# Sigmoid attention and token/channel mixer on one core: accumulating the first batch's token sums in PSUM, laying x back by DMA, permuting on GpSimd, and PSUM banks kept in two-bank tiles

## Chip, cores and metric

One core of one Trainium2 chip. The metric is the device time of one execution in microseconds. With one core, a run over 1.5% above the fastest of the same kernel counts as slow. The span of a profile is about 2 us shorter than the time of that run (398.9 for one of 400.8 before).

Engine names: PE is the TensorE matmul, PEld its weight load, DVE VectorE, ACT ScalarE, POOL GpSimd, SPq the queue of SyncE that issues the plain and the transposing DMAs. POOL issues the loads that cast from float32 to float16.

## The reference, cut to what matters

```python
# q, k, v: (8 batches, 12 heads, 448 tokens, 64); float32
scores = matmul(q, k.T) / 8 - log(448)
attn   = 1 / (1 + exp(-scores))
x      = heads side by side of matmul(attn, v)         # (8, 448, 768)
h      = relu(x.T @ w_tok1) @ w_tok2                   # along tokens, 448 -> 256 -> 448
u      = x + h.T
out    = u + relu(u @ w_ch1) @ w_ch2                   # along channels, 768 -> 1536 -> 768
```

Attention of a later batch and the mixer of an earlier one run side by side, so that PE, which has most of the work, always has some.

## The kernel before: the parts that matter here

A planner in the kernel simulates all engines, picks an order, and then emits the instructions in that order, which gives a list for each engine. A buffer is a `Buf`; it has a few slots, and each slot gets one tile:

```python
    def ap(self):
        if self.tile is None:
            pool = self.plan.pools[self.space]
            self.tile = pool.tile(
                self.shape, self.dtype, tag=f"{self.tag}{self.slot}", bufs=1, name=self.name
            )
        return self.tile
    ...
    def bank(name, shape, dtype=FP32):                       # four single PSUM banks, tag "m"
        return plan.buf("m", 4, shape, dtype, "psum", name)
    ...
    # scores: two slots of two banks
    ps = plan.buf("qk", 2, [128, 2, 512], FP32, "psum", ...)
```

A load brings four heads as rows of 448 elements, heads `2h+s` on partition half `s`:

```python
    nc.gpsimd.dma_start(
        out=t.ap().rearrange("r h j e -> r h (j e)"),
        in_=src[b, 4 * m : 4 * m + 4].rearrange("(h s) (p j) e -> (s p) h (j e)", s=2, j=J),
    )
```

The attention output comes out transposed. PE lays it back, eight 128x128 transposes for each group of four heads ("B"), and DVE copies the result to x. For batch 0, the token mixer (`K1`, relu, `K2`), the add to x, and a PE transpose ("U") lead to `uT`, the input of the first channel matmul ("C1"):

```python
    def back(pb=pb, xt=xt):
        for s in range(2):
            for jj in range(4):
                ...
                nc.tensor.transpose(out=pb[:, jj, :, s, :], in_=xt[:, s, c : c + 128], identity=ident[:, :])
    ...
    # C1: six matmuls of 448 columns into one bank, then a relu by DVE that empties the bank
    nc.tensor.matmul(out=ps[:, :], lhsT=w_ch1[...], rhs=uT[b][:, db, :], start=(db == 0), stop=(db == NDB - 1))
    nc.vector.tensor_scalar(out=h2aT[b][:, cb, :], in0=ps[:, :], scalar1=0.0, scalar2=None, op0=MAX)
```

## Time and profile before

| | before |
|---|---|
| time, median of the runs beside the changed kernel | 402.95 us (401.63 to 406.11) |
| span of the profile | 398.9 us |
| PE busy | 371.8 us, 93% |
| first score matmul | 9.6 us |
| first channel matmul (C1) | 42.8 us |
| PE waits for DVE, summed over the table of waits | 0.9 us |

From the page of the kernel before. Part 1 gives busy time and share of the span; part 2 cuts the span into 40 slices, where a digit is the busy share in tenths:

```profile
PE 371.8 (93%) x3368; PEld 197.1 (49%) x3368; DVE 181.1 (45%) x416; ACT 213.6 (54%) x271; POOL 63.4 (16%) x95
...
PE   2898999199799999999999999999999999999995
...
DMA  7969999978934598548845798638321252031143
```

The dip of PE in slice 8 is the one long stop after the start. The table of PE's waits names it, in the first line here (us in total, times, longest). Slice 11, at seven tenths, holds a shorter stop of 1.9 us, for the tail cast (ACT's float16 copy of `u_tail`, the last 64 tokens of u).

```profile
PE qk L416 <- DMA qT<-qp: 8.6, 1, 8.6
PE tk L371 <- DMA k<-in_k_dram: 7.1, 3, 5.1
```

The DMA queues (packets, MB, share of 16 engines' span), and one line of the windows (us, then busy time of PE, PEld, DVE, ACT and POOL with instruction counts, granted clock, DMA share, GB/s):

```profile
q0 software_dynamic: 24112, 21.93, 35.9%
q1 hardware_dynamic: 54784, 23.41, 30.0%
```

```profile
200.00:250.00 50.00, 50.00 (x443) 26.42 (x442) 21.53 (x53) 29.24 (x38) 6.42 (x9) 1.00 0.75 136
```

PE is busy for 50 of 50 us there, at a DMA share of 0.75. A share of 1 is not the most that this count can reach: from 70 to 80 us it was 1.28.

### The profile page before, as it was taken

Reading aid. Unit: us, or ns where it says so; the run is one execution under the profiler, and the core shown is the slowest. Engines: PE = TensorE matmul, PEld = TensorE weight load, DVE = VectorE, ACT = ScalarE, POOL = GpSimd, SP = SyncE. Lnnn points to the kernel's source line nnn. Section 1 sums busy time; section 2 is a strip of 40 time slices with the busy share of each in tenths; the row PEclk is TensorE's granted clock in tenths of the full one; section 3 lists DMA queues with packets and bytes.
Section 4 is the critical chain, followed back from the end, with each engine's and each line's share of the span. In section 5 each row is a group of like instructions: output and inputs, shape, how many; then the busy total and the mean of one; then the engine's idle time right before and its main releaser. Section 6 shows DMA issues by size and latency. Waiting matters only on the chain.

```text
span 398.9 us, 8001 instructions
## 1 busy us (share of the span) xinstructions
PE 371.8 (93%) x3368; PEld 197.1 (49%) x3368; DVE 181.1 (45%) x416; ACT 213.6 (54%) x271; POOL 63.4 (16%) x95
## 2 busy tenths in 40 slices
PE   2898999199799999999999999999999999999995
PEld 1555454055445554455455554545454554555553
DVE  3377545146544434464442544463342432755321
ACT  1996774167655756586634758476646764220000
POOL 8393325002202022202220012200000000000000
PEclk9999999799999999999999999999999999999999
DMA  7969999978934598548845798638321252031143
GB/s 106 204 102 205 208 208 200 194 112 124 165 63 76 111 197 152 89 88 155 128 73 124 121 187 167 103 67 129 70 48 39 62 114 58 19 63 29 39 109 90
DMA packets 78931, 45.83 MB, mean 115 GB/s; under 512 B 52528, under 2 KB 75248, under 8 KB 78896
## 3 DMA queue, kind: packets, MB, share of 16 engines
q0 software_dynamic: 24112, 21.93, 35.9%
q1 hardware_dynamic: 54784, 23.41, 30.0%
q8 instruction: 26, 0.43, 0.4%
q14 instruction: 9, 0.07, 0.1%
HBM read 43.84 MB, written 11.01 MB: 138 GB/s over the span
## 4 chain that ended last, share of the span: by engine, by line
PE 84%; DMA 10%; POOL 3%; issue 1%; ACT 1%; DVE 0%; POOLq 0%; ACTq 0%
PE c L710 28%; PE c L742 24%; PE qk L416 9%; PE xa L447 7%; PE yn L647 5%; PE k L549 5%; PE c L751 4%; DMA qT<-qp 4%; DMA k<-in_k_dram 3%; PE xb L485 2%; DMA w_tok_s<-in_moe_w_tok_dram 2%; DMA v<-in_v_dram 2%; POOL k L265 1%; POOL w_tok L301 1%; POOL q L265 1%
## 5 line engine op out<-in xcount | busy, mean ns | idle before, releaser
L431 ACT ACTIVATE attn<-qk,att_bias 128x896 f16<-128x896 f32 x168 | 161.5, 1007 | 94.4 <-PE qk L416 94.3
L710 PE MATMUL c<-uT,w_ch 128*128 128x448 f16 x576 | 118.8, 353 | 0.0
L742 PE MATMUL c<-w_ch,h2aT 128*128 128x384 f16 x576 | 100.7, 329 | 0.0
L722 DVE TENSOR_SCALAR h2aT<-c 128x448 f16<-128x448 f32 x96 | 59.9, 624 | 79.8 <-PE c L710 79.6
L710 PEld LDWEIGHTS <-w_ch 128*128 128x128 f16 x576 | 53.0, 98 | 55.5 <-issue 11.9
L742 PEld LDWEIGHTS <-h2aT 128*128 128x128 f16 x576 | 55.8, 99 | 40.9 <-issue 5.6
L416 PE MATMUL qk<-qT,kT 64*64 64x448 f16 x672 | 51.9, 370 | 10.9 <-DMA qT<-qp 8.6
L766 DVE TENSOR_TENSOR u<-u,c 128x384 f32<-128x384 f32 x48 | 26.6, 554 | 65.6 <-PE c L742 65.4
L265 POOL DMA_DIRECT2D v<-in_v_dram x24 | 17.2, 719 | 179.0 <-PE xa L447 164.7
L447 PE MATMUL xa<-attn,v 64*64 64x448 f16 x672 | 36.3, 350 | 0.0
L474 ACT ACTIVATE xT<-xa 128x448 f16<-128x448 f32 x43 | 21.1, 545 | 23.4 <-PE xa L447 23.4
L416 PEld LDWEIGHTS <-kT 64*64 64x64 f16 x672 | 14.4, 105 | 37.6 <-issue 35.4
L447 PEld LDWEIGHTS <-v 64*64 64x64 f16 x672 | 19.4, 107 | 12.9 <-issue 2.6
L659 DVE TENSOR_TENSOR u<-x,yn 128x384 f32<-128x384 f16 x42 | 21.5, 550 | 5.6 <-PE yn L647 5.6
L647 PE MATMUL yn<-h,w_tok 128*128 128x384 f16 x112 | 23.5, 328 | 0.0
L549 PE MATMUL k<-x,w_tok 128*128 128x384 f16 (+1 forms) x102 | 21.2, 318 | 0.0
L669 ACT ACTIVATE u<-u 128x768 f16<-128x768 f32 x21 | 17.6, 845 | 5.5 <-DVE u L659 5.5
L566 ACT ACTIVATE h<-k 128x384 f16<-128x384 f32 (+1 forms) x30 | 14.4, 484 | 9.8 <-PE k L549 9.8
L265 POOL DMA_DIRECT2D q<-in_q_dram x24 | 17.3, 719 | 9.6 <-PE xa L447 3.3
L265 POOL DMA_DIRECT2D k<-in_k_dram x24 | 17.3, 721 | 8.6 <-DMA w_ch<-in_moe_w_ch_dram 6.9
L394 DVE COPY qp<-q 128x384 f16<-128x384 f16 (+1 forms) x54 | 10.9, 266 | 14.4 <-DMA qT<-qp 9.5
L549 PEld LDWEIGHTS <-w_tok 128*128 128x128 f16 x136 | 12.2, 98 | 10.8 <-issue 4.5
(58 smaller groups left out, 192.2 us busy)
## 6 DMA issues: line engine op xcount, KB each, us to landing
out_dram<-u SPq DMA_DIRECT2D x48, 192.0 KB, 2.9
k<-in_k_dram POOLq DMA_DIRECT2D x24, 224.0 KB, 6.0
q<-in_q_dram POOLq DMA_DIRECT2D x24, 224.0 KB, 7.0
v<-in_v_dram POOLq DMA_DIRECT2D x24, 224.0 KB, 4.7
w_ch<-in_moe_w_ch_dram POOLq DMA_DIRECT2D x6, 768.0 KB, 16.4
out_dram<-ut SPq DMA_DIRECT2D x8, 192.0 KB, 2.9
uT<-u SPq DMA_TRANSPOSE x24, 2.8
kT<-kp SPq DMA_TRANSPOSE x18, 3.1
```

The source lines that it names most:

```text
L265: nc.gpsimd.dma_start(out=t.ap().rearrange("r h j e -> r h (j e)"), in_=src[b, 4 * m : 4 * m + 4].rearrange("(h s) (p j) e -> (s p) h (j e ...
L416: nc.tensor.matmul(out=ps[64 * s : 64 * s + 64, h, 0:S], lhsT=kT[64 * h : 64 * h + 64, i, s, :], rhs=qT[64 * h : 64 * h + 64, :, s, :], st ...
L431: nc.scalar.activation(out=at[:, :, :], in_=ps[:, :, 0:S], func=SIGMOID, bias=bias_t[:, :], scale=att_scale,)
L447: nc.tensor.matmul(out=ps[s][64 * h : 64 * h + 64, :], lhsT=vf[64 * s : 64 * s + 64, h, order[i], :], rhs=attn[i][64 * s : 64 * s + 64, h, :],
L474: nc.scalar.activation(out=xt[:, s, :], in_=ps[s][:, :], func=COPYF)
L549: nc.tensor.matmul(out=ps[:, :], lhsT=w_tok1[:, slot, 128 * t : 128 * t + 128], rhs=XT[b][:, c] if jj == 3 else X[b][:, jj, c], start=(jj ...
L647: nc.tensor.matmul(out=ps[:, :], lhsT=w_tok2[:, t, s0 : s0 + 2, :], rhs=h1[:, t, c], start=(t == 0), stop=(t == 1),)
L659: nc.vector.tensor_tensor(out=utile[rows, c] if blk == 3 else u[b][:, blk, c], in0=XT[b][rows, c] if blk == 3 else X[b][:, blk, c], in1=ps ...
L710: nc.tensor.matmul(out=ps[:, :], lhsT=w_ch1[cb // 4][:, db, 128 * (cb % 4) : 128 * (cb % 4) + 128], rhs=uT[b][:, db, :], start=(db == 0), ...
L722: nc.vector.tensor_scalar(out=h2aT[b][:, cb, :], in0=ps[:, :], scalar1=0.0, scalar2=None, op0=MAX)
L742: nc.tensor.matmul(out=ps[:, :], lhsT=h2aT[b][:, cb, 128 * blk : 128 * blk + 128], rhs=w, start=(cb == 0), stop=(cb == NCB - 1),)
L766: nc.vector.tensor_tensor(out=t, in0=t, in1=ps[:, :], op=ADD)
```

## The change

It is meant to shorten the start and to take work from PE and DVE:

- Batch 0: the token sums are matmuls that go on accumulating on the attention output in PSUM (`start=False`), so that one copy gives `uT`. The plain `u` of batch 0 is made later.
- Batches 2 to 7: x is laid back by two transposing DMAs per four heads, issued from SP.
- The permutes of q and k (copies that reorder token groups, before a DMA transposes them) move from DVE to GpSimd, the spreading of `w_tok2` (copies into the layout that K2 reads) from GpSimd to DVE, the token relus from ACT to DVE.
- Batch 0 is loaded in pieces, by head of a pair; turns (the PE transposes of q and k) and scores of the very first heads are cut by head too.
- The planner gets a model of how late DMAs are, and one store of eight PSUM banks that serves pairs ("wide") and single banks.

```diff
+    def banks(self, pool, kept):
+        pair = self.slot // 2
+        if pair not in kept:
+            kept[pair] = pool.tile([128, 2, 512], FP32, tag=f"banks_{pair}", bufs=1, name=f"banks_{pair}")
+        if self.tag == "wide":
+            self.tile = kept[pair]
+            return self.tile
+        t = kept[pair][:, self.slot % 2, :]
+        ...
+            first, n = (6, 7, 5, 4) if self.spare or self.wide == 2 else (6, 7), 1
+        ...
+                b.slot = min(got, key=lambda x: (max(x[0], t), x[1]))[2]
@@ load_qkv, batch 0
+            view = heads.rearrange("(s h) (p j) e -> h s p (j e)", s=2, j=J)
+            for h in range(2):
+                    nc.gpsimd.dma_start(out=t[:, h, :, :].rearrange("r j e -> r (j e)"), in_=view[h])
@@ turned / attention
-                            nc.vector.tensor_copy(out=pm[:, to, :, :], in_=src[:, fr, :, :])
+                    nc.gpsimd.tensor_copy(out=pm[:, to, :, :], in_=src[:, fr, :, :])
+            if b >= 2:
+                for s in range(2):
+                        nc.sync.dma_start_transpose(out=X[b][:, :, cols[s]], in_=xt[:, s, :])
+                continue
@@ batch 0
+                        nc.tensor.matmul(out=ps[s](every), lhsT=h1[0][:, t, ...], rhs=w_tok2[:, t, 0:J, :],
+                            start=False, stop=(t == 1), skip_group_check=True)
... (most of the diff is cut)
```

## The prediction

> **What bounds it now.** The page's engine totals and slices show TensorE (PE) at 93% busy, ACT 54%, DVE 45%, POOL 16%, and the chain of waits is 84% PE work. From 104 to 394 us PE never stops (windows: 80.0 of 80 us, 100.0 of 100 us), so there only removed PE work counts. Time is lost in three places:
> - 0 to 43 us. First score matmul at 9.6 us, first channel matmul at 42.8 us. At warm rates from the chain (8 scores 0.50 us, 28 value matmuls 1.32, 8 transposes 0.45) its PE work is about 27 us, so 16 us are waits. ACT sets the pace to 31 us (21 sigmoids of 1.0 us); then PE waits for k loads until 32.4 and 40.7.
> - 64 to 78 us: PE waits 8.6 us for the transposed q of batch 2 (the table of waits), late because loads saturate the DMA (share 1.2 from 30 to 80 us). The DMA was idle at 20 to 30 us (0.67): POOL waited 4.4 us for w_tok2 and spread it for 3.7 us before issuing more loads.
> - 100 to 104 us: about 2 us for the tail cast of batch 1.
>
> **What the change does.**
> 1. Batches 2 to 7 no longer lay x back with PE: 18 groups of 8 transposes at 0.45 us = -8.1 us, nearly all on the critical path. DVE loses 18 x (0.55 + 0.28) = 15 us, off path. Instead 36 SP transposes of 128x512 run; scaled from the present 128x896 ones (SP issue 1.3 us, landing 3 us): about 0.8 us issue, 2 to 4 us landing. Mean DMA share rises from 0.65 to about 0.72 in the middle: affordable.
> 2. Batch 0: K2, add, PE transpose, copy become 12 matmuls of 448 columns accumulating on the attention output, then one copy. PE: -24 at about 0.11 us, -24 transposes (1.35 us), +12 x 0.19, +16 x 0.16 later (the plain sums, filled in behind): about +1 us. Latency from last sigmoid to first channel matmul falls by 2 to 3 us. [...]
> 3. Start: half loads put the first score near 7.5 us (-2). Spread moves to DVE, so POOL keeps issuing; loads of weights and batch 2 land about 5 us earlier, and the new model of DMA lateness places batch 2's scores later. I expect first channel matmul near 36 us, startup waits -5 us, and the 8.6 us wait nearly gone (-7.5).
> 4. Permutes: 25 us leave DVE (off path); on POOL, by its present copies (784 ns at 128x384, 381 ns at 128x128), 1.95 us each, 70 us over 36: POOL to 30 to 35%. Off path.
> 5. Token relus ACT to DVE: may ease the 2 us at 100 us (-1).
>
> **Sum.** -8.1 - 7.5 - 5 - 1 + 1 = about -20.5; give back 1 for late x transposes: 398.9 to about 379.5 us span, time 382 us (time exceeds span by 2.9 now).
>
> Range 375 to 392. Faster by over 2%: 0.94; within: 0.05; slower: 0.01.
>
> **Right or wrong.** Right if PE busy falls to about 360 us; first score 7 to 8 us; first channel matmul 34 to 38; no wait over 3 us for qT; no K1 wait on x transposes; POOL near 130 us busy. Wrong if bursts of loads and X transposes queue on SP so that K1 or scores wait, or if POOL permutes delay later load issues.

## More of the kernel before

The timeline at the first channel matmuls (start, duration, engine, what; in brackets the idle time of that engine before it, and what ended it):

```profile
42.77 2.44 PE L710 MATMUL c<-uT,w_ch 128*128 128x448 f16 x12
...
44.12 0.62 DVE L722 TENSOR_SCALAR h2aT<-c 128x448 f16<-128x448 f32 x1 [0.57 <-PE c L710]
...
45.15 0.57 PE L416 MATMUL qk<-qT,kT 64*64 64x448 f16 x8
...
45.26 0.62 DVE L722 TENSOR_SCALAR h2aT<-c 128x448 f16<-128x448 f32 x1 [0.51 <-PE c L710]
...
45.55 1.49 PE L447 MATMUL xa<-attn,v 64*64 64x448 f16 x28
```

Two chains of six matmuls fill two banks. The first relu starts at 44.12 us, as soon as the first chain is done and while the second still runs. PE goes on without a bracket: it waits for nothing.

## The result

| | before | after |
|---|---|---|
| time, median | 402.95 us | 507.58 us (505.76 to 510.10) |
| ratio, fast runs | | 1.2587, 95% interval 1.2489 to 1.2684 |
| span | 398.9 us | 505.8 us |
| PE busy | 371.8 us, 93% | 393.2 us, 78% |
| first score, first channel matmul | 9.6, 42.8 us | 13.2, 57.0 us |
| PE waits for DVE | 0.9 us in 2 waits | 77.8 us in 122 waits |

A ratio is the mean time of one kernel's fast runs over that of the other's of the same rounds, so not quite the ratio of the medians that are quoted. The changed kernel was slower by a quarter where a gain of 5% had been forecast.

The lines of the page of the changed kernel that answer to those above:

```profile
PE 393.2 (78%) x3204; PEld 203.2 (40%) x3204; DVE 157.0 (31%) x294; ACT 209.1 (41%) x253; POOL 109.9 (22%) x206
...
PE   1888888887877967797779976987788986966774
...
DMA  7999999948884995689534995262213431210123
```

After the start, where the first turn comes at 9.0 us, no stop is longer than 4.4 us. PE is at seven or eight tenths in nearly every slice: the loss is spread evenly, so it comes from something that happens all the time. The waits of PE say what:

```profile
PE banks L839 <- DVE h2aT L864: 30.9, 44, 0.9
PE banks L481 <- DMA k<-in_k_dram: 9.7, 2, 9.0
PE banks L884 <- DVE u L908: 8.8, 14, 0.7
PE banks L560 <- DVE h2aT L864: 7.2, 10, 0.7
PE banks L839 <- DMA uT<-u: 7.1, 3, 4.4
```

Matmuls of every kind wait some 0.7 us for a DVE operation that empties a bank. L839 is C1, L884 the second channel matmul, L560 the value matmul; a value matmul has no data from `h2aT`, so that wait can only be for room. The timeline at the first channel matmuls:

```profile
59.60 2.43 PE L839 MATMUL banks<-uT,w_ch 128*128 128x448 f16 x12 [0.74 <-DVE h2aT L864]
61.96 0.57 PE L524 MATMUL banks<-qT,kT 64*64 64x448 f16 x8
62.07 1.16 DVE L864 TENSOR_SCALAR h2aT<-banks 128x448 f16<-128x448 f32 x2 [2.52 <-PE banks L839]
...
63.28 2.43 PE L839 MATMUL banks<-uT,w_ch 128*128 128x448 f16 x12 [0.74 <-DVE h2aT L864]
```

Compare with the same place before. The relu of the first chain does not start when that chain is done (about 60.8 us, half of the 2.43 us), but when both are, at 62.07, after 2.52 us of idleness; and the next pair of chains waits until both relus are done. DVE is no slower (622 ns a relu, 624 before) and much idler. Two banks work in lockstep that have nothing to do with each other.

PE's busy time also rose, by 21.4 us with 164 fewer matmuls. Two runs below account for parts of it: with own tiles it is 13.2 us less (e1: 380.0 us), and without the cut by head 7.6 us less again (e13: 373.9 us, e10: 381.5 us).

The DMA queues, and the first loads (out<-in, KB each, median us from issue to landing):

```profile
q0 software_dynamic: 40384, 21.99, 33.7%
q1 hardware_dynamic: 74368, 28.13, 29.6%
...
k<-in_k_dram POOLq DMA_DIRECT2D x6, 112.0 KB, 8.5
```

The same bytes of loads take 16,272 packets more, and the halves of batch 0, at 112 KB, take longer than the 224 KB loads before (median 6.0 us for k).

### The profile page after: what moved, and what is told of

It is laid out like the page before. It is cut to its first block, busy times and chain, and to the rows that moved or that the text cites. A ratio compares the mean times of both kernels' runs of the same rounds, so it can differ in the third digit from the quotient of the medians.

```text
span 505.8 us, 7716 instructions
## 1 busy us (share of the span) xinstructions
PE 393.2 (78%) x3204; PEld 203.2 (40%) x3204; DVE 157.0 (31%) x294; ACT 209.1 (41%) x253; POOL 109.9 (22%) x206
## 4 chain that ended last, share of the span: by engine, by line
PE 61%; DVE 20%; DMA 11%; ACT 3%; issue 3%; POOL 1%; DVEq 0%; POOLq 0%
PE banks L839 24%; PE banks L884 18%; DVE h2aT L864 10%; PE banks L560 6%; PE banks L762 4%; DVE u L908 4%; DMA uT<-u 4%; PE banks L732 3%; DVE u L783 3%; PE banks L893 2%; DMA w_tok<-in_moe_w_tok_dram 2%; DMA k<-in_k_dram 2%; DMA v<-in_v_dram 2%; PE banks L524 2%; DMA x<-xT 2%
## 5 line engine op out<-in xcount | busy, mean ns | idle before, releaser
L539 ACT ACTIVATE attn<-banks,att_bias 128x896 f16<-128x896 f32 (+1 forms) x172 | 161.7, 987 | 128.9 <-PE banks L524 128.5
L839 PE MATMUL banks<-uT,w_ch 128*128 128x448 f16 x576 | 124.6, 359 | 44.4 <-DVE h2aT L864 30.9
L884 PE MATMUL banks<-w_ch,h2aT 128*128 128x384 f16 x576 | 100.7, 326 | 15.2 <-DVE u L908 8.8
L864 DVE TENSOR_SCALAR h2aT<-banks 128x448 f16<-128x448 f32 x96 | 58.4, 622 | 140.8 <-PE banks L839 108.8
L839 PEld LDWEIGHTS <-w_ch 128*128 128x128 f16 x576 | 56.1, 99 | 107.6 <-issue 65.8
L884 PEld LDWEIGHTS <-h2aT 128*128 128x128 f16 x576 | 55.9, 97 | 57.6 <-issue 22.5
L524 PE MATMUL banks<-qT,kT 64*64 64x448 f16 x672 | 55.0, 375 | 1.9 <-ACT attn L539 1.8
L908 DVE TENSOR_TENSOR u<-u,banks 128x384 f32<-128x384 f32 x48 | 26.1, 551 | 87.5 <-PE banks L884 45.0
L560 PE MATMUL banks<-attn,v 64*64 64x448 f16 x672 | 39.4, 361 | 12.9 <-DVE h2aT L864 7.2
L593 ACT ACTIVATE xT<-banks 128x448 f16<-128x448 f32 x43 | 21.6, 543 | 60.9 <-PE banks L839 32.8
L560 PEld LDWEIGHTS <-v 64*64 64x64 f16 x672 | 23.2, 109 | 27.0 <-issue 19.0
L762 PE MATMUL banks<-h,w_tok 128*128 128x384 f16 x128 | 27.6, 326 | 7.7 <-DVE u L783 5.2
L783 DVE TENSOR_TENSOR u<-x,banks 128x384 f32<-128x384 f16 x48 | 24.8, 550 | 25.9 <-PE banks L762 15.2
L732 PE MATMUL banks<-x,w_tok 128*128 128x384 f16 x112 | 20.5, 326 | 6.3 <-DVE h L744 2.5
```

The source lines that it names most:

```text
L524: nc.tensor.matmul(out=ps[64 * s : 64 * s + 64, h, 0:S], lhsT=kT[64 * h : 64 * h + 64, i, s, :], rhs=qT[64 * h : 64 * h + 64, :, s, :], st ...
L539: nc.scalar.activation(out=at[:, hs, :], in_=ps[:, hs, 0:S], func=SIGMOID, bias=bias_t[:, :], scale=att_scale,)
L560: nc.tensor.matmul(out=ps[s](slice(64 * h, 64 * h + 64)), lhsT=vf[64 * s : 64 * s + 64, h, order[i], :], rhs=attn[i][64 * s : 64 * s + 64, ...
L732: nc.tensor.matmul(out=ps[:, :], lhsT=w_tok1[:, w1_slot(side, blk), 128 * t : 128 * t + 128], rhs=X[b][:, x_block(side, blk), c], start=(b ...
L762: nc.tensor.matmul(out=ps[:, :], lhsT=w_tok2[:, t, s0 : s0 + 2, :], rhs=h1[b][:, t, c], start=(t == 0), stop=(t == 1),)
L783: nc.vector.tensor_tensor(out=to, in0=x, in1=y, op=ADD)
```

## The experiments

The same kernel before ran beside each set of experiments on the same chip. Theory A: the diff puts two single banks into one tile, and waits are placed by tile, so neighbours wait for each other. Rivals: B, the plan takes the last used bank again instead of the one free longest, so two of four banks do the work; C, late DMAs or slow permutes. The program itself, listed with its waits, supports A before any run. DVE's list in the changed kernel has

```
86 L864 TensorScalarPtr h2aT_1381<-banks_89 128x448
87 L864 TensorScalarPtr h2aT_1381<-banks_89 128x448 [waits PE_49]
88 L864 TensorScalarPtr h2aT_1381<-banks_89 128x448
89 L864 TensorScalarPtr h2aT_1381<-banks_89 128x448 [waits Activation_49]
```

A relu without a wait needs none, because the one before waited for both banks; the last one waits for ACT, which had only read the neighbour. In the whole list, 24 of the 96 relus have no wait, 5 wait for ACT and 67 for PE, and 88 read the same pair of banks (counted in the program that the kernel builds). With own tiles (e1) all 96 wait for PE.

### e1: own tiles for single banks

```diff
-        pair = self.slot // 2
-        ...
-        t = kept[pair][:, self.slot % 2, :]
+        if self.tag != "wide":
+            one = ("one", self.slot)
+            if one not in kept:
+                kept[one] = pool.tile([128, 512], FP32, tag=f"bank_{self.slot}", bufs=1, name=f"bank_{self.slot}")
+            t = kept[one][:, :]
```

> The changed kernel, same plan and same bank numbers, but each single PSUM bank is its own tile; only score pairs keep a two-bank tile. Theory A (two banks in one tile are synchronised as one, so an eviction waits for the neighbour's matmuls and the next matmuls wait for both evictions): the PE waits for DVE evictions, some 70 us in the changed kernel, fall below 20 us and the time falls to 385 to 415 us. Theory B (the plan takes the same bank again as soon as it is thought free, so two of four banks do all the work): little changes, over 470 us. Theory C (transposing DMAs, POOL permutes or loads are late): over 480 us.

Measured: 422.83 us, ratio to before 1.0532 (1.0457 to 1.0607), result correct. The plan and its bank numbers are those of the changed kernel. PE's waits for DVE fell from 77.8 us in 122 to 0.7 us in 2; the largest waits that are left are for DMAs:

```profile
PE bank L485 <- DMA k<-in_k_dram: 11.2, 3, 9.3
PE bank L843 <- DMA uT<-u: 11.0, 3, 5.5
PE banks L528 <- DMA qT<-qp: 3.7, 1, 3.7
```

From 1.2587 to 1.0532 of the time before is some 83 us of 403 (two sets of rounds). The shared tile is the cause of most of the loss; e2 shows what made it so large. The time was some us above the range that theory A gave, since the rest is not its doing.

### e2: rotate the banks, tiles still shared

```diff
-                b.slot = min(got, key=lambda x: (max(x[0], t), x[1]))[2]
+                b.slot = min(got, key=lambda x: (x[0], x[1]) if b.tag == "bank" else (max(x[0], t), x[1]))[2]
```

> The changed kernel, still paired tiles, but the plan takes the bank that has been free longest, so all four banks rotate. Theory A with both causes needed: the pairs take turns, so most of the waits go, 410 to 460 us. Theory A alone with pairing as the whole cause: above 470 us. Theory B: 385 to 410 us. Theory C: no change, over 490 us.

Measured: 443.73 us, ratio 1.1069 (1.1000 to 1.1137). PE's waits for DVE fell to 17.7 us in 44. The likely reading is that PE fills one pair while DVE empties the other. Rotation alone takes back 15 of the 26 points, some 61 us, own tiles alone 21. So the damage of the shared tile was as large as it was because the plan kept to one pair. It is the case "both needed".

### e3: own tiles and rotation

> Both at once: own tiles and rotation. Theory A and B together: as the first of these runs or up to 10 us less, 375 to 405 us. Theory C: over 480 us.

The edit is e1 and e2 together. Measured: 423.42 us, ratio 1.0473 (1.0373 to 1.0573; two of four runs slow), no different from e1. With own tiles the choice of bank does not matter, so B alone is out. The range that was expected for the time was again too low.

### e4: the kernel before, with its single banks put two to a tile

```diff
+            if self.tag == "m":
+                pair = self.slot // 2
+                ...    # one [128, 2, 512] tile for each pair, as in the change
+                self.tile = t = self.plan.kept[pair][:, self.slot % 2, :]   # cut: bitcast, reshape
+                return t
             self.tile = pool.tile(
```

> The kernel before, plan untouched, with its four single banks put two to a tile. Theory A (pairing is enough by itself): 440 to 500 us, with PE waits for DVE evictions that the kernel before has not. Theory B or C: within 2% of the kernel before, about 402 us, because its bank choice already takes the bank free longest.

Measured: 432.58 us, ratio 1.0766 (1.0690 to 1.0842). Pairing alone, with plan and order of the kernel before, costs 31 us by the ratio; B and C had expected none. It is a little less than the 440 us foreseen, perhaps because this plan takes the bank that is free longest, as e2 does (5.4 points above e1). The profiled run was slow, so only its kind of wait is used here: PE waits for DVE rose from 0.9 to 15.8 us, for ACT from 3.3 to 10.3.

With a tile for each single bank, e1 gave correct results, and all 96 relus wait for PE. So in this case a guard over two banks is wider than needed.

### e5: batch 0 loaded in long rows

```diff
-            view = heads.rearrange("(s h) (p j) e -> h s p (j e)", s=2, j=J)
-            for h in range(2):
-                    nc.gpsimd.dma_start(out=t[:, h, :, :].rearrange("r j e -> r (j e)"), in_=view[h])
+            for s in range(2):
+                    nc.gpsimd.dma_start(
+                        out=t[64 * s : 64 * s + 64, :, :, :].rearrange("r h j e -> r h (j e)"),
+                        in_=heads[2 * s : 2 * s + 2].rearrange("h (p j) e -> p h (j e)", j=J))
-                need = [lds[h]] if len(lds) > 1 else lds
+                need = lds
```

This and all that follow, but for e12, stand on e1; e8 to e11 and e13 to e16 contain this edit too.

> Own tiles for single banks, and the loads of the first batch are cut by token halves of the partitions (rows of 896 bytes, one piece per partition and head) instead of by head pairs; as many loads, as many bytes. Theory P (the head-pair cut falls apart into about 1,030 packets per load against about 256 for a load twice as large before, which slows the start): packets of the software queue fall by about 16,000, the first score comes at 9 to 10 us instead of 12.8, the first channel matmul 5 to 8 us earlier, time 5 to 10 us below own tiles alone, 413 to 418 us. Theory Q (the start is late because POOL issues more and smaller loads): under 2 us.

Measured: 410.15 us, ratio 1.0129 (1.0015 to 1.0243), so 4 points below e1 by the ratios, which come from two sets of rounds, and 4 below e7 (1.0555), which is as fast as e1 and ran in the same rounds. As many loads and bytes, but

```profile
q0 software_dynamic: 24256, 21.93, 37.9%
...
k<-in_k_dram POOLq DMA_DIRECT2D x6, 112.0 KB, 4.5
```

The packets are back at the old number. In the window from 10 to 20 us, the DMA moved 185 GB/s at a share of 1.18, against 107 GB/s at 1.25 in e1: just as busy, with less to show. First score at 10.0 us (12.8 in e1), first channel matmul at 48.6 (53.0). Theory P holds, though its sizes were off: the time fell by about 16 us and not 5 to 10, the first channel matmul by 4.5 us and not 5 to 8. Q is out, as the number of loads is the same. 18 loads of 112 KB with about 1,030 packets each, in place of 256 for twice the size, were slower: the median landing of k was 8.6 us in e1 and is 4.5 us here. Why the short packets are slower was not measured.

### e6: x of batches 2 to 7 laid back by PE again

```diff
-            if b >= 2:
+            if b >= 99:
                 for s in range(2):
                     ... nc.sync.dma_start_transpose(out=X[b][:, :, cols[s]], in_=xt[:, s, :])
```

> Own tiles, and x of batches 2 to 7 is laid back by PE transposes and DVE copies as before; 36 transposing DMAs fewer. Theory T (they queue on SP so that the u transposes come late and PE stops, and those stops cost more than the PE work saved): PE waits for u fall from 11 us to under 3, PE work rises 8 us, time 415 to 423 us. Rival (the x transposes are a plain gain of 8 us): time 8 us above own tiles alone, about 430 us.

Measured: 413.98 us, ratio 1.0254 (1.0167 to 1.0341), 2.8 points below e1 of other rounds and 3.0 below e7 of the same. The part of the change that was to save 8 us costs about 11 in this plan, a little more than theory T said. PE waits for `uT` (11.0 us in e1) are gone from the table, and PE's busy time rises by 4.2 us (384.2 from 380.0), not by 8.

### e7: permutes back on DVE

```diff
-                    nc.gpsimd.tensor_copy(out=pm[:, to, :, :], in_=src[:, fr, :, :])
+                    nc.vector.tensor_copy(out=pm[:, to, :, :], in_=src[:, fr, :, :])
```

> Own tiles, and the permutes of q and k are back on DVE. Theory (off the critical path on both engines): within 2 us of own tiles alone, 420 to 425 us. Rival (permutes on POOL hold back loads and qT): 5 us or more faster.

Measured: 426.19 us, ratio 1.0555 (1.0460 to 1.0650); e1 has 1.0532. The intervals lie over each other. Where the permutes run does not show in the time. The waits do shift: PE waits 9.0 us for DVE (0.7 in e1), 6.4 of them at once, and no longer 3.7 us for q by DMA.

### e8: one x transpose in place of two

On e5. The two 128x512 transposes of a head group become one of 128x1024 into a differently laid out x; matmul and add read x through a matching view (the diff is some 30 lines of addressing).

```diff
-                for s in range(2):
-                        nc.sync.dma_start_transpose(out=X[b][:, :, cols[s]], in_=xt[:, s, :])
+                    flat = X[b].ap().rearrange("t a d -> t (a d)")[:, 1024 * m : 1024 * m + 1024]
+                    nc.sync.dma_start_transpose(out=flat.rearrange("t (z c) -> t z c", c=128),
+                                                in_=xt.ap().rearrange("r s c -> r (s c)"))
```

> As the first run here, and the two x transposes of 128x512 of each head group are one of 128x1024. Theory T (an SP transpose costs about 1.25 us to issue whatever its size, so halving the count frees SP): SP issue time of x falls from 45 to about 25 us, waits of PE for u and x fall by half, time 5 to 10 us below the first run here. Rival (what counts is the bytes through the transposing DMA): same as the first run here.

Measured: 410.94 us, ratio 1.0157 (1.0076 to 1.0237), the same as e5. PE waits for `uT` were 16.3 us (13.1 in e5). One issue takes 1.24 us (median) at 128x1024 and 1.22 at 128x512, so SP's issue time for x fell from about 45 to 25 us as theory T said. It gained nothing, so this issue time was not the limit; the rival's outcome came.

### e9: a late-bound name

Copies that should go to ACT only for the last head group of batch 0 test `last` when they are emitted, when it is always true. So they run on ACT for all three groups while the plan counts them on DVE.

```diff
-                def lay(pb=pb, cols=cols, s=s):
+                def lay(pb=pb, cols=cols, s=s, last=last):
   ... the same for relu and keep
```

> Own tiles, long load rows, and a late-bound name is mended: in the changed kernel the copies of x, of the first-batch relu and of the sums that go to ACT only for the last head group go to ACT for all three groups, although the plan counts them on DVE. Theory (about 3 us of work sits on ACT, in order, where ACT sets the pace of the start): first channel matmul 2 to 4 us earlier than 48.6, time 2 to 4 us less than without, 406 to 408 us against 410. Rival (start is set by loads): no change within 1 us.

Measured: 410.21 us, ratio 1.0229 (1.0176 to 1.0282), against 1.0129 for e5 on another chip, with overlapping intervals. First channel matmul at 46.5 us in place of 48.6, but no gain in time can be seen: a miss. The mended form is kept in what follows.

### e10: e9 with x laid back by PE

> The same with x of batches 2 to 7 laid back by PE and DVE. Theory T (late transposing DMAs stop PE[...]): 8 to 12 us less than the run without, 395 to 400 us, so at or just below the kernel before. Rival: 8 us more, as the PE work says.

The edit is that of e6. Measured: 401.57 us, ratio 1.0028 (0.9970 to 1.0087), 2.0 points below e9 of the same rounds, about 8 us. Theory T holds again, at the low end of its 8 to 12 us. With tiles, rows, and x put back, the kernel is level with the one before. The timeline of e9 shows what one late transpose costs:

```profile
146.07 1.23 SPq L823 DMA_TRANSPOSE uT<-u  x1
...
153.62 4.64 PE L843 MATMUL bank<-uT,w_ch 128*128 128x448 f16 x12 [6.49 <-DMA uT<-u]
```

The chain of waits of e9 puts 7.42 us between issue and landing of this DMA. PE stands for 6.49 us, and then twelve matmuls that take 2.43 us elsewhere take 4.64. The page of e9 gives a granted clock of seven tenths for that slice (153.4 to 163.6 us), nine or more for most others. Stop and slow matmuls together cost 8.70 us, about a third more than the stop alone. Twelve of these matmuls were also slow after the stops of 5.55 us in e1 (4.64 us) and of 7.02 us in e5 (3.94 us); after one of 1.80 us in e1, six took 1.31 us, as elsewhere.

### e11: a plan that knows how late transposes are

```diff
                 o.end = t + 3.0 + min(5.0, max(0.0, self.pipe - t - 0.5))
+                if o.name[:2] != "st":
+                    self.turns = max(self.turns, t + 0.8) + 2.2
+                    o.end = max(o.end, self.turns + 0.6)
```

> The first run here with x still laid back by DMA, but the plan counts the transposes as one serial line of 2.2 us each, as the traces show in bursts, in place of a fixed 3.0 us, so that it places the first channel matmuls of a batch later. Theory T2 (the loss lies in the order that the plan made, not in the DMAs): PE waits for u fall from 13 to under 4 us, time 395 to 402 us. Rival (the DMAs cannot keep up): waits move to other places, 405 to 412 us.

The 2.2 us can be read in e1, where two `uT` transposes in a row held SP for 4.45 us (from 150.43 us) and for 4.13 us (from 195.75 us).

Measured: 406.04 us, ratio 1.0128 (1.0066 to 1.0191), one point below e9. Waits for `uT` fell from 14.4 to 2.6 us, but waits for x rose from 1.7 to 5.5 and those of the scores for ACT from 2.4 to 5.2. That is half of what e10 gains. The time lies in the range of the rival, and waits moved to other places as it said; of theory T2 only the fall of the waits for `uT` came true. The order was part of the loss, not all of it.

### e12: the kernel before, with the spreading of w_tok2 on DVE

```diff
-                nc.gpsimd.tensor_copy(out=w_tok2[...], in_=src[...])
+                nc.vector.tensor_copy(out=w_tok2[...], in_=src[...])
-        c = op("spread", "POOL", 4.0, spread, ...)
+        c = op("spread", "DVE", 1.7, spread, ...)
```

> The kernel before with one part of the change alone: the spreading copies of w_tok2 on DVE, so that POOL goes on issuing loads. If step 3 of the prediction is right, loads land about 5 us earlier, and the 8.6 us wait for q of batch 2 shrinks: 394 to 399 us against 402. If it is wrong: within 2 us of the kernel before.

Measured: 400.20 us, ratio 0.9984 (0.9928 to 1.0041). The DMA share from 20 to 30 us rises from 0.67 to 1.25 as I had argued, yet the wait for q of batch 2 only falls from 8.6 to 6.6 us. PE reaches that point earlier too (it stops at 67.5 us, 69.4 before), and loading goes on: the DMA share from 60 to 80 us is 1.38. This is the outcome that the expectation had named for "wrong": no gain from this step by itself can be seen.

### e13: no cut by head

Two terms were open then: why the start is not shorter, and whether the saving by x transposes can be had at all. The turns and scores of batches 0 and 1 are joined: both heads of a pair transposed in turns, into both halves of the columns.

```diff
-        parts = [range(2)] if (b, m) != (0, 0) else [range(1), range(1, 2)]
+        parts = [range(2)]
-            for h in hs:
-                    for i, j in enumerate(ORDER[side]):
-                        nc.tensor.transpose(out=ps[64 * h : 64 * h + 64, i, :, :], ...)
+                    for i, j in enumerate(ORDER[side]):
+                        for h in range(2):
+                            nc.tensor.transpose(out=ps[64 * h : 64 * h + 64, i, :, :], ...)
-            if (b, m) == (0, 0):
+            if False:
                 both = [(i, (0,)) for i in range(SPLIT)] + ...
```

> As e10 (own tiles, long rows, x by PE), and the turns and scores of batches 0 and 1 are no longer cut by head: both heads of a pair are transposed side by side in one group. Theory (a cut turn uses half of the PE columns: 7 transposes take as long as 14 side by side): turns of 14 take 0.6 us where two cut ones take 1.1, first channel matmul 3 to 6 us earlier, 396 to 399 us against 401.6. Rival (the start is set by loads): under 1 us.

Measured: 399.40 us; two of four runs were slow, and the two fast runs are 397.42 and 394.98 us beside 402.82 for before. First channel matmul at 40.2 us (48.0 in e10). That is more than the 3 to 6 us expected. Turns of e5, cut by head, and then of e16, which has the same joined turns as e13, both early, while PE is slow (later, fourteen take 0.58 us in e13):

```profile
12.29 0.95 PE L485 MATMUL bank<-ident,k 128*64 128x128 f16 x7
13.17 0.58 PE L528 MATMUL banks<-qT,kT 64*64 64x448 f16 x2
13.68 0.95 PE L485 MATMUL bank<-ident,q 128*64 128x128 f16 x7
```

```profile
7.08 0.96 PE L489 MATMUL bank<-ident,k 128*64 128x128 f16 x14 [7.08 <-DMA k<-in_k_dram]
7.80 0.99 PE L489 MATMUL bank<-ident,q 128*64 128x128 f16 x14
```

Fourteen transposes that alternate between the halves of the array take as long as seven in one half, 0.96 and 0.95 us. The cut that was to start ACT sooner doubled PE's time where PE was the limit: from 10 to 17 us, PE never waits in e10 after its first score, while ACT waits for it four times, 0.4 to 0.8 us each, and is busy for 6.5 of the 10 us from 10 to 20 us. The rival, that the loads set the start, is out, since the loads are the same. The edit joins turns and scores together, so their shares are not known.

### e14, e15, e16: all, half and none of x by DMA, with the mended start and the honest plan

e14 is e11 with the edit of e13. e15 lays back only odd batches by DMA (`if b >= 2 and b % 2:`). e16 is e13 with the plan of e11.

> As e11 (x by DMA, plan with a serial line of transposes), and no cut by head. 3 to 6 us below e11: 400 to 403 us. If the DMA is at its capacity in the middle, PE waits for u and x stay at 5 us or more.

> As the run before, but only odd batches lay x back by DMA, even ones by PE. Capacity theory: half of the transposes fit, so PE waits for u and x go below 3 us while 4 us of PE work are saved: 393 to 397 us, the best of the four. Order theory (the plan was the trouble): no better than the run with all x by DMA.

> As the first run here, with the plan's serial line of transposes. x by PE throughout, so the DMA has room: within 2 us of the first run, 395 to 399 us.

| | x by DMA | median | ratio to before (95%) | PE busy from 100 to 300 us | DMA share, 200 to 250 us |
|---|---|---|---|---|---|
| e14 | all | 399.02 us | 0.9872 (0.9762 to 0.9982) | 190.1 us | 1.01 |
| e15 | odd batches | 401.14 us | 0.9967 (0.9892 to 1.0042) | 193.2 us | 0.90 |
| e16 | none | 397.66 us | 0.9801 (0.9665 to 0.9937) | 197.1 us | 0.79 |

The busy times are summed over four windows of 50 us of each profile. The windows from 200 to 250 us of e14 and of e16:

```profile
200.00:250.00 50.00, 46.03 (x404) 23.63 (x401) 18.29 (x33) 27.35 (x33) 15.05 (x30) 1.00 1.01 152
```

```profile
200.00:250.00 50.00, 50.00 (x461) 26.36 (x460) 20.64 (x40) 30.76 (x37) 13.46 (x27) 1.00 0.79 135
```

With all of x by DMA, PE idles 7.0 us more in these 200 us than with none. In them it was spared 112 of the 144 transposes, some 6 us, so the idling eats that up. Half gives half the idleness, and no better time. The capacity theory asked for PE waits for `uT` and x of 5 us or more in e14, and there were 6.3, but also for less than 3 in e15, and there were 6.0. So "half would fit" is refuted, and the honest plan does not bring the saving either. Whether a better order would, or DMA capacity forbids it, stays open. e14 came out 1 us below its range, e16 in its range, within 2 us of e13. e16 has the lowest median: about 2% below the kernel before (the interval is a gain of 0.6 to 3.4%, so the verdict at 2% is "unclear"; two of its four runs counted as slow), and about 22% below the changed kernel (0.9801 over 1.2587). Its interval and that of e14 lie over each other.

## Why the prediction was wrong, point by point

- **The step that failed** is in "What bounds it now": that in the middle "PE never stops", "so there only removed PE work counts". It took for granted that the changed kernel leaves PE as free to run ahead as before. I had read the new bank store, with its two-bank tiles, and gave it no term in the sum. e1 measures the term: about 83 us, with 77.8 us of PE waits for DVE in place of 0.9. e2 shows that it takes two things together, the two-bank tile and a plan that stays with one pair of banks: rotation alone takes back some 61 us. e4 shows that the same edit hurts the kernel before as well.
- **Step 3, the start** ("half loads put the first score near 7.5 us", first channel matmul "near 36 us", -5): wrong in sign. It was 13.2 and 57.0 us. Loads torn into short rows (e5, about 16 us of time) and turns cut by head (e13, 8 us of the first channel matmul) were in the diff and not costed. With both mended, and own tiles, e16 has 9.5 and 39.5 us.
- **Step 3, the spread**: the mechanism was right (DMA share at 20 to 30 us from 0.67 to 1.25 in e12), its worth was not: 2 us of the 8.6 us wait, nothing in the total.
- **Step 1, x by DMA**: the 144 transposes did leave PE (192 of 128x128 before, 48 after). I took 0.8 us issue, 2 to 4 us landing and a DMA share of 0.72. In e9, issue has a median of 1.22 us and landing 5.3 us (2.4 to 9.1), and from 200 to 250 us the share was 0.89. By e10 the term is a loss of 8 us in that plan and by e14 to e16 no gain in the best one. I had named the danger ("bursts of loads and X transposes queue on SP") and given it 1 us.
- **Step 2, sums on the attention output**: it works: the attention output is read in mid-group and added to afterwards, and the outputs of all experiments that contain this (all but e4 and e12) were correct. From the last sigmoid of batch 0 to the first channel matmul, the kernel before takes 12.0 us (30.7 to 42.8) and e13 takes 10.4 (29.8 to 40.2). That is 1.6 us, of "2 to 3" forecast. Other work lies between, and the part was not run alone, so this is only an indication.
- **Step 4, permutes**: right that they are off the path, as far as the time tells (e7). Their size was off: 510 and 296 ns a copy, 1.3 us for three in place of 1.95, and POOL was busy for 110 us and not 130.
- **Step 5, relus**: the 1.9 us wait for the tail cast is gone in e1, whose table of waits has no line for it. It was not tested alone.

## What to carry to other kernels

Before moving buffers into one larger tile, ask what the waits are placed by: here, two independent PSUM banks in one tile turned a free-running pipeline into a lockstep, and the sign was short idle times (122 of some 0.6 us) before matmuls of every kind, on PE and DVE in turn, with no DVE operation slower. Ask also how many of the buffers the plan really uses. When a load or a transposition is cut into pieces, count what a piece becomes, in packets (here about 1,030 in place of 256 for twice the size) and in parts of the array used (here seven transposes in one half in 0.95 us, fourteen in both in 0.96), and not only its bytes. Work taken off the busiest engine gained nothing here where what replaced it came late (e9 took 8 us more than e10); compare idle time in the same window, not only busy time.

## Further figures from the runs

- A tile over two PSUM banks was guarded as one. Here that cost a ratio of 1.2587 against 1.0532 (e1), and 1.0766 when put into the kernel before (e4).
- 36 transposing DMAs of 128x512 in float16 (4.7 MB) add to the hardware queue 36.8% of 409.1 us less 29.7% of 402.6 us, which is 31 us of all 16 engines (e9 and e10). An estimate from this is 152 GB/s; it was taken beside other traffic. Landing had a median of 5.3 us.
- A permuting copy of 128x384 in float16 took 510 ns on POOL (changed kernel) and 286 to 302 ns on DVE (kernel before), and the spreading copy of the same size 784 ns on POOL (kernel before).
- In the changed kernel a load of 112 KB became about 1,030 packets (of 112 bytes on average) although rows of 896 bytes stood contiguous in it.
